# Gate factors made on TensorE, x loaded in three mirrored transfers, masters in blocks of four

## The chip, the cores and the metric

The kernel runs on one core of one Trainium2 chip. The metric is the device time of one launch in microseconds (us). Before the change it is 581.54 us, the median of three runs from 579.77 to 585.35. The profiled run took 580.86 us, and its profile spans 578.8 us from the first to the last instruction.

The engines are called by the profile's short names: PE is TensorE (PEld its weight loads), DVE is VectorE, ACT is ScalarE, POOL is GpSimd, SP is SyncE, which here only issues DMAs (SPq).

## The reference

Two computations on the same x (2048 tokens, 448 features) are mixed by a gate. The first is attention with 16 query heads of 28 and one shared key and value head. The second is a convolution of each feature with a long kernel K that is built from 256 complex modes per feature.

```python
g = sigmoid((x * gate_w).sum(-1, keepdims=True))
# A: attention
q = (x @ wq) in 16 heads of 28;  k = x @ wk;  v = x @ wv
p = softmax(q k^T * 28**-0.5);   a = (p v, heads side by side) @ wo
# B: long convolution
P = exp(dt * A * l), l = 0 .. 2047            # 448 x 256 modes x 2048 positions
K = Re sum_n C[d,n] * dt[d] * B[d,n] * P      # 448 x 2048
b = causal_conv(x, K) per feature, in bf16, + x * Dskip
out = g * a + (1 - g) * b
```

## The kernel before

The program is written as a list of operations with their reads and writes. A scheduler in the Python code orders them per engine with assumed durations (`ns`), priorities (`pr`, lower first) and a `slack` that is added to the assumed arrival of an operand. The order of each engine is then fixed in the program. An engine stalls where the next instruction of its own list isn't ready, even if a later one is.

**Attention.** 1024 score tiles of 128x512 (4 query blocks x 4 head groups x 16 key tiles x 4 heads) come in batches of 3 and 2. PE makes a batch of scores (line 938), ACT takes its exponential (948), PE multiplies with the values (956).

```python
for b in range(nb):                       # nb = 410 batches, 2.5 tiles on average
    if b >= nextc and c < NCH + LAG:
        chunk_step(c)                     # masters, tables(c), kgen(c), conv(c - LAG); LAG = 2
        c += 1; nextc += period
    ...pv(npv)...
    if b + 2 < nb:
        qk(b + 2)
```

After 16 key tiles, `norm` divides by the sum of exponentials. The sums go through DRAM to be spread over partitions: acc (a DVE copy of psB) to denT by DMA, a reciprocal on DVE, denT to R_scratch by DMA, R_scratch to rdenB by four DMAs, and a DVE product into onT. The output projection (885) reads onT.

**Convolution.** The 448 features are 28 chunks of 16. For each chunk DVE builds tables of powers from "masters" (`tables`), PE contracts them to K (`kgen`, 803), DVE packs K into kstg, and a DMA writes it to KP_scratch. Four DMAs of 1 MB (`tload`) read it back as overlapping windows, the Toeplitz data T, in a ring of four slots. PE then multiplies T with U, which holds x in blocks of 64 tokens in reversed block order (`conv`, 864: 128 matmuls for a chunk). DVE scales the result by omq, which is 1 - g in the layout of the reversed convolution, and PE transposes it (842).

```python
def uload(self):
    pg.dma([(U rows 16.., dram(self.Z, ...))], (448, 2048), "uz", rd=["pad", "sw"], wr=["U"], pr=2)   # zeros
    for k in range(3):
        lst = []
        for p in range(16):
            if k == 0: hb, pos, blk = 0, p, 15 - p
            else:      hb, pos, blk = 1, p + 16 * (k - 1), 31 - p - 16 * (k - 1)
            lst.append((U[partitions hb, hb+2, .., 64 of them; columns pos*D .. pos*D+D],
                        dram(x, 64 * blk * D, [[D, 64], [1, D]])))
        pg.dma(lst, (1024, 896), f"u{k}", rd=["sw"], wr=["U"], pr=2)     # 16 DMAs each

def conv(self, c):
    for k in range(4):
        self.tload(4 * c + k)
        for m in range(1, 16, 2):
            pg.op("pe", mm, 112, rd=[("T", s), "U"], ..., slack=2500 if m == 1 else 0)
    pg.op("dve", cst = ps * omq, rd=[X, "omq"]);  self.ytr(c)
```

Every write of U names the same resource, so each of the four groups (zeros, u0, u1, u2) is issued only when the one ahead of it has landed. U is complete only after the last.

**Masters.** For a block of BC chunks, 11 levels of repeated squaring: a copy and a signed copy to bf16 at each level (738, 740), and a square, a subtraction and a product from each level to the next (728, 731, 734). That is 22 + 30 DVE instructions for a block, whatever its size.

```python
sizes = [2, 4, 4, 4, 4, 4, 4, 2]
pr = 50 + c0 if b else 1.4          # masters of the block that starts at chunk c0
# tables of chunk c have pr = 52 + c
```

**Gate operand.** gtok holds g and 1 - g by token. The copy for the convolution's layout goes through DRAM:

```python
pg.op("dve", gb = bf16(1 - g))
pg.dma([(dram(self.G, 0, [[1, P], [P, 16]]), gb)], (2048, 2), "gw", ..., slow=True)   # 2048 elements of 2 bytes
pg.dma([(tq, dram(self.G, 0, [[64, 32], [1, 64]]))], (32, 128), "omq", rd=["G"], wr=[("kst", 1)])
pg.op("pe", mo, 200, rd=["anti", ("kst", 1)], wr=[("b", 5)], slack=6000)   # 2 selector matmuls
pg.op("dve", omq = copy of the result)
```

Of the kernel before, what the change touches and what calls it, by code (L numbers as in the profile page):

```python
# [44 lines left out]
def dram(t, off, dims):  # L45
    return bass.AP(tensor=t.tensor, offset=t.offset + off, ap=[list(d) for d in dims])
# [244 lines left out]
def el(n, rate=0.96, fix=69):  # L291
    return fix + n / rate


class Kernel:
# [4 lines left out]
    def sb(self, name, cols, dt):  # L300
        return Buf(self.es.enter_context(self.nc.sbuf_tensor(name, [P, cols], dt)))
# [23 lines left out]
    def alloc(self):  # L325
        nc = self.nc
        sb = self.sb
        self.psS = self.ps("psS", 3072)
        self.psB = self.ps("psB", 512)
        self.psX = self.ps("psX", 512)  # L330
        self.psSb, self.psBb, self.psXb = self.psS.cast(BF), self.psB.cast(BF), self.psX.cast(BF)
        self.xT = sb("xT", NT * S, BF)
        self.kT = sb("kT", S, BF)
        self.vaug = sb("vaug", 512, BF)
        self.Wq = sb("Wq", NT * 512, BF)
        self.Wk = sb("Wk", NT * P, BF)
        self.Wv = sb("Wv", NT * 32, BF)
        self.Wo = sb("Wo", NT * D, BF)
        self.Wb = sb("Wb", P, BF)
        self.ident = sb("ident", 136, BF)  # L340
        self.absq = sb("absq", 512, BF)
        self.qT = sb("qT", 3 * 512, BF)
        self.expT = sb("expT", 10 * 512, BF)
        self.acc = sb("acc", 2 * 512, F32)
        self.rdenB = sb("rdenB", 512, F32)
        self.denT = sb("denT", 2 * 16, F32)
        self.onT = sb("onT", 6 * 512, BF)
        self.gtok = sb("gtok", 32, F32)
        self.gb = sb("gb", 16, BF)
        self.dskb = sb("dskb", D, BF)  # L350
        self.omq = sb("omq", 128, F32)
        self.anti = sb("anti", 2 * P, BF)
        self.U = sb("U", 32 * D, BF)
        self.O = sb("O", 16 * D, BF)
        self.tab = sb("tab", 2 * 8192, BF)
        self.tmp = sb("tmp", 2 * 2048, BF)
        self.NTR = 4
        self.T = sb("T", self.NTR * 4096, BF)
        sizes = [2, 4, 4, 4, 4, 4, 4, 2]
        self.blocks = [(sum(sizes[:i]), n) for i, n in enumerate(sizes)]  # L360
        self.NB = len(sizes)
        self.BC = max(sizes)
        self.LV = 192
        self.MC = 5 * 192 + 96
        self.mbf = sb("mbf", 2 * self.BC * self.MC, BF)
        BW = self.BC * HC
        self.BW = BW
        self.mst = sb("mst", 2 * 2 * BW, F32)
        self.msq = sb("msq", 2 * BW, F32)
        self.sgn = sb("sgn", 8, F32)  # L370
        self.seedz = sb("seedz", 2 * 2 * D, F32)
        self.seedw = sb("seedw", 2 * 2 * D, BF)
        self.dt32 = sb("dt32", D, BF)
        self.kstg = sb("kstg", 2 * 256, BF)
        self.cst = sb("cst", 2 * 512, BF)
        self.small = sb("small", 32, F32)
        self.zero = sb("zero", 2, BF)
        self.smallb = sb("smallb", 16, BF)
        self.KP = nc.dram_tensor("KP_scratch", (D * KPW,), BF).ap()
        self.Z = nc.dram_tensor("Z_scratch", (1024,), BF).ap()  # L380
        self.G = nc.dram_tensor("G_scratch", (S,), BF).ap()
        self.R = nc.dram_tensor("R_scratch", (16 * 4 * 512,), F32).ap()

    def consts(self):
# [12 lines left out]
        ms = lambda buf, n, val, key, eng="dve": pg.op(eng, lambda e: e.memset(V(buf, 0, n), val), 60 + n / 3.8, wr=[key])  # L397
        pg.op("dve", lambda e: e.memset(V(self.kstg, 0, 256), 0.0), 100, wr=[("kst", 0)])
        ms(self.Wk, NT * P, 0.0, "Wk")
        ms(self.Wq, NT * 512, 0.0, "Wq")  # L400
        ms(self.Wb, P, 0.0, "Wb")
        for hb in range(4):
            pg.op("dve", lambda e, hb=hb: e.memset(self.Wb.v(32 * hb, 28, 32 * hb + 28, [[1, 1]]), -1.0), 60, wr=["Wb"])
        pg.op("dve", lambda e: e.memset(self.vaug.v(0, P, 28, [[32, 16]]), 1.0), 80, wr=["va"])
        pg.op("dve", lambda e: e.memset(self.vaug.v(0, P, 29, [[32, 16], [1, 3]]), 0.0), 80, wr=["va"])
        ms(self.Wo, NT * D, 0.0, "Wo", "pool")
        for z in range(2):
            an = self.anti.v(0, 32, z * P, [[32, 4], [1, 32]])
            pg.op("pool", lambda e, an=an: e.memset(an, 1.0), 100, wr=["anti"], pr=4)
            pg.op("pool", lambda e, an=an, z=z: e.affine_select(out=an, in_=an, compare_op=ALU.is_equal, fill=0.0, base=z - 32,  # L410
                                                                pattern=[[0, 4], [1, 32]], channel_multiplier=1), 300,
                  rd=["anti"], wr=["anti"], pr=4)

    def loads(self):
# [61 lines left out]
    def uload(self):  # L476
        pg, x = self.pg, self.ins["A_x"]
        pg.dma([(bass.AP(tensor=self.U.h, offset=16 * D, ap=[[2 * self.U.rs, 64], [1024, 7], [1, 1024]]),
                 dram(self.Z, 0, [[0, 64], [0, 7], [1, 1024]]))], (448, 2048), "uz", rd=["pad", "sw"], wr=["U"], pr=2)
        for k in range(3):  # L480
            lst = []
            for p in range(16):
                if k == 0:
                    hb, pos, blk = 0, p, 15 - p
                else:
                    hb, pos, blk = 1, p + 16 * (k - 1), 31 - p - 16 * (k - 1)
                lst.append((bass.AP(tensor=self.U.h, offset=hb * self.U.rs + pos * D, ap=[[2 * self.U.rs, 64], [1, D]]), dram(x, 64 * blk * D, [[D, 64], [1, D]])))
            pg.dma(lst, (1024, 896), f"u{k}", rd=["sw"], wr=["U"], pr=2)

    def bank(self, b, bf=False):  # L490
        if b < 6:
# [142 lines left out]
    def prep_gate(self):  # L634
        pg = self.pg
# [15 lines left out]
        pg.op("dve", lambda e: e.tensor_scalar(gv, ov, 0.5, 0.5, ALU.mult, ALU.add), 80, rd=["gt"], wr=["gt"], pr=1.2)  # L651
        pg.op("dve", lambda e: e.tensor_scalar(ov, ov, -0.5, 0.5, ALU.mult, ALU.add), 80, rd=["gt"], wr=["gt"], pr=1.2)
        pg.op("dve", lambda e: e.tensor_copy(self.gb.v(0, P, 0, [[1, 16]]), ov), 80, rd=["gt"], wr=["gb"], pr=1.2)
        pg.dma([(dram(self.G, 0, [[1, P], [P, 16]]), self.gb.v(0, P, 0, [[1, 16]]))], (2048, 2), "gw", rd=["gb"], wr=["G"], pr=3, slow=True)
        tq = self.kstg.v(0, 32, 256, [[1, 64]])
        pg.dma([(tq, dram(self.G, 0, [[64, 32], [1, 64]]))], (32, 128), "omq", rd=["G"], wr=[("kst", 1)], pr=1)
        t, o = self.bank(5)

        def mo(e):
            for z in range(2):  # L660
                r = e.matmul(t.v(0, P, o + 64 * z, [[1, 64]]), self.anti.v(0, 32, z * P, [[1, P]]), tq,
                             start=True, stop=True, tile_position=(0, 0))
            return r
        pg.op("pe", mo, 200, rd=["anti", ("kst", 1)], wr=[("b", 5)], pr=1.7, slack=6000)
        pg.op("dve", lambda e: e.tensor_copy(self.omq.v(0, P, 0, [[1, 128]]), t.v(0, P, o, [[1, 128]])), el(128),
              rd=[("b", 5)], wr=["omq"], pr=1.7)

# [22 lines left out]
    def masters(self, b):  # L690
        pg = self.pg
# [1 line left out]
        BW, MC, B0 = BC * HC, self.MC, c0 * HC  # L693
        W2 = 2 * D
        mo = (b % 2) * self.BC * MC
        pr = 50 + c0 if b else 1.4
        mst, msq, mbf = self.mst, self.msq, self.mbf

        def src(k, comp):
# [152 lines left out]
    def conv(self, c):  # L852
        pg = self.pg
# [3 lines left out]
        for k in range(4):  # L857
# [3 lines left out]
            for m in range(1, 16, 2):  # L861
                def mm(e, k=k, m=m, s=s, gi=gi):
                    for j in range(4):
# [4 lines left out]
                    return r  # L868
                first = k == 0 and m == 1
                pg.op("pe", mm, 112, rd=[("T", s), "U"], wr=[X, ("cst", cs)] + ([("b", 5)] if c == 0 else []) if first else [X], pr=2.5,  # L870
                      lock="C" if first else None, slack=2500 if m == 1 else 0, mode="c32")
        pg.op("dve", lambda e: e.tensor_tensor(self.cst.v(0, P, cs * 512, [[128, 4], [64, 2], [1, 64]]),  # L872
                                               ps.v(0, P, po + 63, [[128, 4], [64, 2], [-1, 64]]),
                                               self.omq.v(0, P, 0, [[0, 4], [64, 2], [1, 64]]), ALU.mult),
# [189 lines left out]
```

## Time and profile before

| what | value |
|---|---|
| time, median of 3 | 581.54 us |
| span of the profile | 578.8 us |
| busy PE / DVE / ACT | 491.5 / 494.6 / 488.9 us |
| exponentials (948) | 410, 472.1 us, 1253 ns each |
| mean granted PE clock | 0.876 |
| DMA moved | 136.6 MB, 236 GB/s over the span |

Three engines are each busy for about 85% of the span. Such shares are averages over a beginning, a long middle and an end with different limits, so the reading goes by stretches of time.

| stretch, us | PE busy | DVE busy | ACT busy | PE clock | DMA share |
|---|---|---|---|---|---|
| 20 to 40 | 14.95 | 17.20 | 17.62 | 0.56 | 0.35 |
| 60 to 80 | 16.54 | 14.88 | 18.49 | 0.67 | 0.31 |
| 80 to 100 | 7.29 | 14.67 | 8.26 | 0.50 | 0.53 |
| 180 to 200 | 17.60 | 20.00 | 20.00 | 1.00 | 0.75 |
| 420 to 440 | 18.05 | 20.00 | 19.70 | 1.00 | 0.92 |
| 540 to 560 | 9.54 | 2.39 | 0.00 | 0.70 | 0.88 |
| 560 to 580 | 6.67 | 4.54 | 0.00 | 0.67 | 0.28 |

### The profile page before, as it was taken

The numbers are of one execution on the slowest core, as the hardware profiler recorded it, in microseconds if no ns is written. First come the engines' busy times: TensorE is split into PE (matmuls) and PEld (weight loads), VectorE is DVE, ScalarE is ACT, GpSimd is POOL, SyncE is SP. The second block draws the span as 40 slices with busy tenths as digits, with TensorE's granted clock in tenths as the row PEclk, the third lists the DMA queues.
The fourth block names the chain that finished last, engine by engine and source line by source line (L and its number), as shares of the span: only waits on it lengthen the run. The fifth ranks groups of instructions, "written<-read, shape, count | busy, mean of one in ns | idle before, by whom it ended". The sixth has DMA issues, their size and how long they took to land.

```text
span 578.8 us, 18479 instructions
## 1 busy us (share of the span) xinstructions
PE 491.5 (85%) x8210; PEld 243.9 (42%) x8210; DVE 494.6 (85%) x1197; ACT 488.9 (84%) x428; POOL 3.7 (1%) x15
## 2 busy tenths in 40 slices
PE   6777962989898999989899999999999989999552
PEld 5411210334444444535345254555544455555431
DVE  4978976799999999999989899999999999992112
ACT  4688891999999999999989799999999989999000
POOL 2000000000000000000000000000000000000000
PEclk9755565779989999979879699999999999989867
DMA  8827336358667778488687667769998868989953
GB/s 227 202 20 58 78 78 203 139 187 310 217 220 297 255 246 286 153 307 296 211 317 213 263 221 255 271 240 337 290 314 298 267 211 324 317 297 302 378 210 127
DMA packets 44847, 136.62 MB, mean 236 GB/s; under 512 B 11516, under 2 KB 27824, under 8 KB 30432
## 3 DMA queue, kind: packets, MB, share of 16 engines
q1 hardware_dynamic: 44032, 135.08, 70.0%
q8 instruction: 64, 1.05, 0.7%
q10 hardware_dynamic: 736, 0.37, 0.2%
q14 instruction: 15, 0.12, 0.1%
HBM read 131.44 MB, written 3.86 MB: 234 GB/s over the span
## 4 chain that ended last, share of the span: by engine, by line
PE 44%; ACT 36%; DMA 9%; DVE 4%; SPq 4%; issue 1%; ACTq 0%
ACT expT L948 35%; PE psS L938 13%; PE psS L864 12%; PE psB L956 8%; PE psX L803 5%; SPq L106 4%; DMA U<-Z_scratch 3%; PE psX L885 2%; PE psX L678 2%; DMA R_scratch<-denT 1%; DMA denT<-acc 1%; PE psS L510 1%; DMA rdenB<-R_scratch 1%; DMA T<-KP_scratch 1%; DVE O L466 1%
## 5 line engine op out<-in xcount | busy, mean ns | idle before, releaser
L948 ACT ACTIVATE expT<-psS 128x1536 bf16<-128x1536 f32 (+1 forms) x410 | 472.1, 1253 | 34.8 <-PE psS L938 19.6
L938 PE MATMUL psS<-qT,kT 29*128 29x512 bf16 x1024 | 174.7, 422 | 36.8 <-ACT expT L948 34.6
L864 PE MATMUL psS<-T,U 128*32 128x128 bf16 (+7 forms) x3584 | 158.4, 303 | 21.1 <-DMA T<-KP_scratch 20.8
L864 PEld LDWEIGHTS psS<-T,U 128*32 128x32 bf16 (+7 forms) x3584 | 114.7, 151 | 56.8 <-issue 27.4
L956 PE MATMUL psB<-expT,vaug 128*32 128x512 bf16 x1024 | 112.0, 428 | 2.3 <-ACT gtok L649 1.3
L938 PEld LDWEIGHTS psS<-qT,kT 29*128 29x128 bf16 x1024 | 39.6, 92 | 135.4 <-ACT expT L948 99.3
L769 DVE TENSOR_TENSOR tab<-tab,mbf 128x128 bf16<-128x128 bf16 (+4 forms) x140 | 78.9, 566 | 0.4
L778 DVE TENSOR_TENSOR tab<-tab,tmp 128x128 bf16<-128x128 bf16 (+4 forms) x140 | 78.5, 566 | 0.4
L772 DVE TENSOR_TENSOR tmp<-tab,mbf 128x128 bf16<-128x128 bf16 (+4 forms) x140 | 78.4, 563 | 0.0
L803 PE MATMUL psX<-tab 128*32 128x96 bf16 x1792 | 58.9, 268 | 2.7 <-issue 2.1
L956 PEld LDWEIGHTS psB<-expT,vaug 128*32 128x32 bf16 x1024 | 26.8, 95 | 68.2 <-issue 63.7
L803 PEld LDWEIGHTS psX<-tab 128*32 128x32 bf16 x1792 | 43.5, 116 | 14.9 <-issue 8.4
L786 DVE TENSOR_TENSOR tab<-tab,mbf 128x2048 bf16<-128x2048 bf16 x28 | 34.1, 1219 | 0.0
L788 DVE TENSOR_TENSOR tab<-tab,mbf 128x2048 bf16<-128x2048 bf16 x28 | 34.0, 1212 | 0.0
L872 DVE TENSOR_TENSOR cst<-psS,omq 128x512 bf16<-128x512 f32 x28 | 19.2, 686 | 13.7 <-PE psS L864 13.7
L740 DVE TENSOR_TENSOR mbf<-mst,sgn 128x256 bf16<-128x256 f32 (+1 forms) x80 | 30.7, 383 | 0.0
L728 DVE TENSOR_TENSOR msq<-mst 128x256 f32<-128x256 f32 (+1 forms) x72 | 27.6, 383 | 0.0
L678 PE MATMUL psX<-xT,Wq 112*128 112x512 bf16 x64 | 24.1, 474 | 0.5 <-DVE qT L687 0.2
L915 DVE TENSOR_TENSOR onT<-acc,rdenB 128x512 bf16<-128x512 f32 x16 | 10.9, 684 | 13.9 <-DMA rdenB<-R_scratch 13.9
L731 DVE TENSOR_TENSOR mst<-msq 128x128 f32<-128x128 f32 (+1 forms) x80 | 21.3, 266 | 0.0
L904 DVE COPY acc<-psB 128x512 f32<-128x512 f32 x16 | 11.0, 688 | 10.3 <-PE psB L956 10.3
L734 DVE SCALAR_TENSOR_TENSOR mst<-mst 128x128 f32<-128x128 f32 (+1 forms) x72 | 19.2, 267 | 0.0
(100 smaller groups left out, 251.3 us busy)
## 6 DMA issues: line engine op xcount, KB each, us to landing
T<-KP_scratch SPq DMA_DIRECT2D x112, 1024.0 KB, 7.9
rdenB<-R_scratch SPq DMA_DIRECT2D x64, 64.0 KB, 3.2
U<-in_A_x_dram SPq DMA_DIRECT2D x48, 56.0 KB, 2.2
tab<-in_A_x_dram SPq DMA_DIRECT2D x4, 448.0 KB, 6.6
O<-in_A_x_dram SPq DMA_DIRECT2D x1, 1792.0 KB, 9.8
KP_scratch<-kstg SPq DMA_DIRECT2D x28, 64.0 KB
out_dram<-O SPq DMA_DIRECT2D x16, 112.0 KB, 1.8
U<-Z_scratch SPq DMA_DIRECT2D x1, 896.0 KB, 15.2
```

The costliest lines, as they stand in the source:

```text
L678: pg.op("pe", lambda e, T=T: e.matmul(px, self.Wq.v(0, DT, T * 512 + g * 128, [[1, 128]]), self.xT.v(0, DT, T * S + 512 * qc, [[1, 512]]), ...
L740: pg.op("dve", lambda e, k=k, io=io, sg=sg: e.tensor_tensor(mbf.v(0, P, mo + io, [[MC, BC], [1, 64]]), src4(k), self.sgn.v(0, P, sg, [[0, ...
L769: pg.op("dve", lambda e, d=dst, a=src, m=m, w=w: e.tensor_tensor(d, a, mbf.v(0, P, m, [[4, 16], [0, 2 * w], [1, 4]]), ALU.mult), el(n, 1.9 ...
L772: pg.op("dve", lambda e, a=src, m=m, w=w: e.tensor_tensor(tmp.v(0, P, so, [[4 * w, 32], [1, 4 * w]]), a, mbf.v(0, P, m + 64, [[4, 32], [0, ...
L778: pg.op("dve", lambda e, d=d2, t=t2: e.tensor_tensor(d, d, t, ALU.add), el(n, 1.92), rd=[("tmp", s), ("tab", s, lv + 1)], wr=[("tab", s, l ...
L786: pg.op("dve", lambda e: e.tensor_tensor(ua, src, mbf.v(0, P, m, [[4, 8], [0, 64], [1, 4]]), ALU.mult), el(2048, 1.92), rd=rk + mk, wr=[(" ...
L788: pg.op("dve", lambda e: e.tensor_tensor(ub, src, mbf.v(0, P, m + 32, [[4, 16], [0, 32], [1, 4]]), ALU.mult), el(2048, 1.92), rd=rk + mk, ...
L803: r = e.matmul(self.psX.v(32 * g, 32, 96 * jj, [[1, 96]]), tab.v(0, P, qp + 2048 + o, [[4, 32]]), tab.v(0, P, to + o, [[2048, 3], [4, 32]] ...
L864: r = e.matmul(ps.v(32 * j, 33 - m, po + 128 * k, [[1, 128]]), self.U.v(0, P, (m - 1) * D + 4 * gi + j, [[D, 33 - m]]), self.T.v(0, P, s * ...
L938: r = e.matmul(self.psS.v(0, P, 1536 * s + 512 * k, [[1, 512]]), kT.v(32 * h, DH + 1, 128 * kt, [[1, 128]]), qT.v(32 * h, DH + 1, 512 * qs ...
L948: pg.op("act", lambda e: e.activation(expT.v(0, P, 512 * (i0 % 10), [[1, n]]), self.psS.v(0, P, 1536 * s, [[1, n]]), AF.Exp, scale=SQ), 75 ...
L956: r = e.matmul(self.psB.v(32 * h, 32, 0, [[1, 512]]), vaug.v(0, P, 32 * kt, [[1, 32]]), expT.v(0, P, 512 * ((4 * st + h) % 10), [[1, 512]] ...
```

## The change

Three things change together.

1. The gate operand no longer goes through DRAM. PE transposes gb (128 x 16) into 16 rows, DVE copies them to kstg, and four selector matmuls (16 rows instead of 32, two halves that accumulate) make omq. Two DMAs fall away. POOL builds four selectors instead of two.
2. The 48 DMAs that load x into U become three, with a block axis that runs backwards through U.
3. The masters come in seven blocks of four instead of eight of 2, 4, ..., 4, 2, and those after the first rank later, just before the tables of their first chunk. In the scheduler, the assumed lateness of T for the first convolution chunk rises from 2.5 to 9 us, so that the chunk is placed later.

```diff
-        self.anti = sb("anti", 2 * P, BF)
+        self.anti = sb("anti", 4 * P, BF)
-        sizes = [2, 4, 4, 4, 4, 4, 4, 2]
+        sizes = [4] * 7
-        self.G = nc.dram_tensor("G_scratch", (S,), BF).ap()
... (consts: four selectors with 16 rows and a row step of 2 instead of two with 32 rows)
+        rs = self.U.rs
         for k in range(3):
-            lst = []
-            for p in range(16):
-                if k == 0:
-                    hb, pos, blk = 0, p, 15 - p
-                else:
-                    hb, pos, blk = 1, p + 16 * (k - 1), 31 - p - 16 * (k - 1)
-                lst.append((bass.AP(tensor=self.U.h, offset=hb * self.U.rs + pos * D, ap=[[2 * self.U.rs, 64], [1, D]]), dram(x, 64 * blk * D, [[D, 64], [1, D]])))
-            pg.dma(lst, (1024, 896), f"u{k}", rd=["sw"], wr=["U"], pr=2)
+            hb, p0, b0 = (0, 15, 0) if k == 0 else (1, 31, 0) if k == 1 else (1, 15, 16)
+            pg.dma([(bass.AP(tensor=self.U.h, offset=hb * rs + p0 * D, ap=[[2 * rs, 64], [-D, 16], [1, D]]),
+                     dram(x, 64 * b0 * D, [[D, 64], [64 * D, 16], [1, D]]))], (1024, 896), f"u{k}", rd=["sw"], wr=["U"], pr=2)
...
-        pg.dma([(dram(self.G, 0, [[1, P], [P, 16]]), self.gb.v(0, P, 0, [[1, 16]]))], (2048, 2), "gw", rd=["gb"], wr=["G"], pr=3, slow=True)
-        tq = self.kstg.v(0, 32, 256, [[1, 64]])
-        pg.dma([(tq, dram(self.G, 0, [[64, 32], [1, 64]]))], (32, 128), "omq", rd=["G"], wr=[("kst", 1)], pr=1)
+        tq = self.kstg.v(0, 16, 256, [[1, P]])
+        tb, ob = self.bank(5, True)
+        pg.op("pe", lambda e: e.matmul(tb.v(0, 16, ob, [[1, P]]), self.gb.v(0, P, 0, [[1, 16]]), self.ident.v(0, P, 0, [[1, P]]),
+                                       is_transpose=True, tile_position=(0, 0)), 100, rd=["gb", "id"], wr=[("b", 5)], pr=1.6)
+        pg.op("dve", lambda e: e.tensor_copy(tq, tb.v(0, 16, ob, [[1, P]])), el(P), rd=[("b", 5)], wr=[("kst", 1)], pr=1.2)
...
             for z in range(2):
-                r = e.matmul(t.v(0, P, o + 64 * z, [[1, 64]]), self.anti.v(0, 32, z * P, [[1, P]]), tq,
-                             start=True, stop=True, tile_position=(0, 0))
+                for half in range(2):
+                    r = e.matmul(t.v(0, P, o + 64 * z, [[1, 64]]), self.anti.v(0, 16, (2 * z + half) * P, [[1, P]]),
+                                 self.kstg.v(0, 16, 256 + 64 * half, [[1, 64]]),
+                                 start=(half == 0), stop=(half == 1), tile_position=(0, 0))
-        pg.op("pe", mo, 200, rd=["anti", ("kst", 1)], wr=[("b", 5)], pr=1.7, slack=6000)
+        pg.op("pe", mo, 300, rd=["anti", ("kst", 1)], wr=[("b", 5)], pr=1.7)
...
-        pr = 50 + c0 if b else 1.4
+        pr = 51.5 + c0 if b else 1.4
... (conv)
-                      lock="C" if first else None, slack=2500 if m == 1 else 0, mode="c32")
+                      lock="C" if first else None, slack=(2500 if gi else 9000) if m == 1 else 0, mode="c32")
```

More of the change, by code (lines that the diff above doesn't have):

```diff
@@ L406, in consts @@
         ms(self.Wo, NT * D, 0.0, "Wo", "pool")
-        for z in range(2):
-            an = self.anti.v(0, 32, z * P, [[32, 4], [1, 32]])
+        for zh in range(4):
+            an = self.anti.v(0, 16, zh * P, [[32, 4], [1, 32]])
             pg.op("pool", lambda e, an=an: e.memset(an, 1.0), 100, wr=["anti"], pr=4)
-            pg.op("pool", lambda e, an=an, z=z: e.affine_select(out=an, in_=an, compare_op=ALU.is_equal, fill=0.0, base=z - 32,
-                                                                pattern=[[0, 4], [1, 32]], channel_multiplier=1), 300,
+            pg.op("pool", lambda e, an=an, zh=zh: e.affine_select(out=an, in_=an, compare_op=ALU.is_equal, fill=0.0,
+                                                                  base=zh // 2 + zh % 2 - 32, pattern=[[0, 4], [1, 32]],
+                                                                  channel_multiplier=2), 300,
                   rd=["anti"], wr=["anti"], pr=4)
```

## The prediction

> **What bounds the kernel now.** I read four views, in this order: the waits by engine, the timelines of SP and PE around the longest of them, the busy times by stretch, and the chain of work at the end.
>
> ```profile
> ACT expT L948 <- PE psS L938: 19.6, 18, 11.6
> SPq L106 <- DMA G_scratch<-gb: 13.0, 1, 13.0
> ```
>
> The columns of the waits are the sum in us, the number and the longest. ACT waited for scores for 19.6 us in all, and 11.6 us of it in one piece. SP stood for 13 us behind the write of the gate to DRAM.
>
> ```profile
> 36.74 0.38 SPq L106 DMA_DIRECT2D G_scratch<-gb  x1
> 39.64 0.67 SPq L106 DMA_DIRECT2D U<-Z_scratch  x1
> 53.38 0.32 SPq L106 DMA_DIRECT2D kstg<-G_scratch  x1
> 54.90 22.35 SPq L106 DMA_DIRECT2D U<-in_A_x_dram  x32
> 77.29 0.68 SPq L106 DMA_DIRECT2D denT<-acc  x1
> 78.75 10.90 SPq L106 DMA_DIRECT2D U<-in_A_x_dram  x16
> 89.69 0.59 SPq L106 DMA_DIRECT2D KP_scratch<-kstg  x1
> 92.22 0.56 SPq L106 DMA_DIRECT2D T<-KP_scratch  x1
> ```
>
> This is SP's timeline (start, duration, instruction). SP is a serial resource here: the gate and the 48 small loads of x keep it from 36.7 to 89.7 us. The first K (KP_scratch) can be written only then, although DVE had packed it at 72.2 us (end of the copy at line 818), and the first T follows.
>
> ```profile
> 86.57 0.61 PE L938 MATMUL psS<-qT,kT 29*128 29x512 bf16 x2
> 98.41 1.22 PE L864 MATMUL psS<-T,U 128*32 128x128 bf16 x32 [11.24 <-DMA T<-KP_scratch]
> ```
>
> In PE's own order the first convolution matmul comes next, and its T isn't there. PE stops, no scores are made, and ACT stops from 88.6 to 100.2 us. This is the hole in the stretch from 80 to 100 us.
>
> ```profile
> 40.00:50.00 10.00, 8.95 (x8) 0.50 0.91 46
> 390.00:400.00 10.00, 9.98 (x10) 1.00 0.95 351
> ```
>
> These are the exponentials by stretch: length, ACT busy, granted PE clock, DMA share, GB/s. From 100 to 536.6 us they fill the time almost wholly: that stretch has about 419 us of them and some 17 us of gaps. The DMA engines at 40 us are as busy as at 390 us, but for an eighth of the bytes: this is the gate's write of 2-byte elements, with the zeros of U beside it.
>
> ```profile
> 537.84 5.65 DMA denT<-acc
> 543.79 7.68 DMA R_scratch<-denT
> 552.30 1.34 SPq L106
> 553.69 6.79 DMA rdenB<-R_scratch
> 560.50 0.70 DVE onT L915
> ```
>
> This is the end of the chain. After the last exponential (536.6 us) 42.2 us remain: three dependent DMAs, which share the queues with the last 1 MB loads of T, then the last projection and the stores.
>
> **What the Trainium skill says.** "DMA: Bandwidth & Descriptors", section Specifications, puts the smallest efficient transfer at 512 B and says that below it a read-modify-write is done. The trace agrees: 4 KB in 2-byte elements held SP for 13.0 us. The same page, section "Issuing engines are not separate DMA queues", says that issuing costs sequencer time, usually small beside the DMA. Here it isn't small: 32 issues took 22.35 us, 0.70 each, for 56 KB that land in 2.2 us. "TensorE: Matmul & The Clock Gate", Part 1, says that the clock is halved until PE has been busy for a window. The trace shows 0.50 to 0.67 before the convolution starts and 1.00 in most later stretches, so that the stretch before the first convolution chunk is slow for PE in both kernels.
>
> **The change part by part.**
>
> *The loads of x.* 48 issues (22.35 + 10.90 us) become three. One load of x into O, 1.8 MB in pieces of the same 896 B, landed in 9.8 us by the table of DMA issues. Half of that with its fixed part is 5 to 6 us, so I estimate 6 us for each of the three, one after the other. With the zeros landed at 54.9 us or earlier, U is complete at about 73 us instead of 91.
>
> *The gate.* Two DMAs and the 13 us wait go. Added are five small matmuls of under 0.5 us each at half clock and one DVE copy of about 0.2 us, at a time when PE waits for ACT anyhow: I count 0.5 us.
>
> *The masters.* By the groups kept apart by shape, a block of two costs 11x0.189 + 11x0.284 + 10x0.284 + 10x0.216 + 10x0.217 = 12.4 us of DVE. A block of four costs 11x0.220 + 11x0.416 + 10x0.416 + 10x0.282 + 10x0.284 = 16.8 us. Two blocks of two go and one of four comes: 8.0 us less in all. But the first block grows by 4.4 us and stands ahead of the first tables. In PE's built order the first K is contracted after score tile 95 instead of 80.
>
> *When the first T is there.* The old hole came after tile 115, with the exponentials reaching 88.6 us. Before it, 36 exponentials ran from 43.42 to 88.61 us, 1.26 us each, or 0.50 us a tile. Tile 95 is thus reached at about 78.5 us. The write of K takes 0.6 us to issue and 2.5 us to land (89.69 to 92.22), four rdenB issues stand beside it (2.3 us), and the first T took 6.2 us from 92.22 to 98.4. So T is there at about 88 us. The convolution now starts after tile 135, which is 20 tiles or 8 exponentials later: 88.6 + 8x1.26 = 98.7 us. It finds U and T ready, with 10 us to spare.
>
> *The middle.* Before, the 909 tiles after tile 115 took 536.6 - 88.6 - 11.6 = 436.4 us, 0.480 us each. At the same pace 889 tiles end at 98.7 + 426.8 = 525.5 us. That is 11.1 us earlier.
>
> *The tail.* The built orders differ here as well. After the last product with the values, 320 convolution matmuls were left, now 256. After the last denT transfer, six loads of T were left, now four, and only one of them, instead of three, stands between R_scratch and the four rdenB. At the 344 GB/s of the stretch from 540 to 560 us a load of 1.05 MB takes 3.05 us, so up to 6.1 us are to be had. The writing of R_scratch still has three loads ahead of it, so I take two thirds, 4 us.
>
> *Sum.* 11.1 for the hole, 4 for the tail, less 0.5 for the added gate work and 0.6 for gaps that move: 14 us. 581.5 - 14 = 567.5 us.
>
> **The rivals.** First, another wait takes the place of the hole. The first K is contracted later, and the loads of U now run as three dependent transfers of 0.9 MB into 64 partitions with a backward axis. If one of these took 15 us, as the zeros did, U would be there only at 100 us, at the planned start of the convolution. For this speaks that nobody has seen that transfer; against it, that the zeros shared the engines with the gate's write. It would give 575 to 581 us. Second, the middle is bound by more than ACT. From 140 to 520 us DVE is idle for about 10 us only and PE for some 25, and the same convolution work must fit into 889 tiles instead of 909. The masters, now placed just before the tables of their first chunk, could make K come in bursts. For it speaks the built order: K for chunks 3 and 4 is contracted at tiles 185 and 245, with 60 tiles between. Against it: DVE has 8 us less work and no longer loses the 9 us (3.80 and 5.33) that it spent before 100 us on denT and rdenB. If the pace fell from 0.480 to 0.490 us, 9 us would go: 575 to 577. Third, the tail is a chain of latencies and doesn't shrink: 571 to 572. In the other direction, if R_scratch also passes sooner and some gaps of the middle close, 560.
>
> **Range and chances.** The hole is the surest part. The tail is worth 0 to 6 us and the middle is uncertain by some 6 us either way. I put 8 in 10 on 559 to 577 us. The line of 2% is at 569.9 us, a little above my value, so: faster 0.63, same 0.33, slower 0.04.
>
> **What would show it.** Right: no wait of ACT above 3 us near 100 us; the first convolution matmul at 96 to 101 us with no DMA as its releaser; SP free of U's loads before 75 us; the last exponential at 523 to 529 us; 37 to 40 us from there to the end; about 486 us of DVE. Wrong: a wait on U or T ahead of the first convolution matmul; more than 22 us of gaps between the exponentials after it; a tail of 42 us or more; or a clock that stays at half after 100 us.

## The result

| kernel | median | range | ratio to before, 95% interval |
|---|---|---|---|
| before | 581.88 us (4 runs) | 579.77 to 585.35 | |
| after | 552.96 us (4 runs) | 552.07 to 554.21 | 0.9499 [0.9448, 0.955] |

The change saves 28.9 us, twice the 14 us that were predicted, and 552.96 us lies below the range of 559 to 577 us. The profiled executions span 578.8 and 552.4 us, so they show 26.4 us of it.

SP's timeline of the kernel after (start, duration, instruction):

```profile
41.20 0.68 SPq L106 DMA_DIRECT2D U<-Z_scratch  x1
49.07 11.41 SPq L106 DMA_DIRECT2D U<-in_A_x_dram  x3
66.71 0.66 SPq L106 DMA_DIRECT2D denT<-acc  x1
...
79.13 0.58 SPq L106 DMA_DIRECT2D KP_scratch<-kstg  x1
79.76 1.86 SPq L106 DMA_DIRECT2D rdenB<-R_scratch  x4
81.72 2.81 SPq L106 DMA_DIRECT2D T<-KP_scratch  x4
```

SP no longer stands behind the gate. The zeros land in 7.9 us by the table of DMA issues instead of 15.2, each of the three loads of x in 5.4 us, and U is complete at about 66 us at the latest (the third is issued by 60.5 us). SP still waits for one load before it issues the next, as the 11.41 us for three issues show. The first K is written at 79.1 us, the four loads of T follow from 81.7. PE's timeline at the first convolution matmul of after:

```profile
96.08 0.39 PE L938 MATMUL psS<-qT,kT 29*128 29x512 bf16 x2
96.40 0.48 PE L864 MATMUL psS<-T,U 128*32 128x128 bf16 x8
```

There is no bracket with a releaser: PE waits for nothing, and the hole is gone. The waits of ACT in the kernel after (sum in us, number, longest):

```profile
ACT expT L948 <- PE psB L956: 9.6, 27, 0.9
ACT expT L948 <- PE psS L938: 3.7, 8, 0.9
```

The wait for scores fell from 19.6 to 3.7 us. That is 4 us more than the 11.6 us of the hole. The waits after 100 us, for scores and for the products with the values (psB), fell as well. First before, then after, both from 100 us to the last exponential (the 11.6 us in the first view are the hole, which ends at 100.2 us):

```profile
ACT expT L948 <- PE psS L938: 17.9, 15, 11.6
ACT expT L948 <- PE psB L956: 9.8, 26, 1.5
```

```profile
ACT expT L948 <- PE psB L956: 7.3, 22, 0.7
ACT expT L948 <- PE psS L938: 0.8, 3, 0.5
```

Without the hole, the 16.1 us of short waits after 100 us became 8.1 us. The groups of instructions say that the exponentials themselves are the same in both kernels; before, then after (busy us, mean ns, idle time ahead of them):

```profile
L948 ACT ACTIVATE expT<-psS 128x1536 bf16<-128x1536 f32 (+1 forms) x410 | 472.1, 1253 | 34.8 <-PE psS L938 19.6
```

```profile
L948 ACT ACTIVATE expT<-psS 128x1536 bf16<-128x1536 f32 (+1 forms) x410 | 470.0, 1252 | 14.2 <-PE psB L956 9.6
```

The chain that ended last, in after (start, duration, work):

```profile
519.69 9.60 DMA R_scratch<-denT
...
531.62 2.15 DMA rdenB<-R_scratch
533.77 0.02 issue
533.79 0.70 DVE onT L915
...
534.54 5.62 PE psS L885 x16
540.16 1.03 PE psS L864 x24
```

The last exponential ends at 514.4 us, and rdenB, which took 6.79 us, now takes 2.15.

The end of the exponentials can be written as a sum for every kernel here: 40 us, ACT's busy time after it (460 to 463 us in all of them), and ACT's idle time. Then comes a tail. I worked out this table from the exponentials' timeline and the busy times by stretch of one profile each; it says where time went, and the medians below say how much. The gaps after 100 us differ by some 3 us between profiles of one order: 12.7 to 15.8 us in hole_closed and in the run that shortens DVE's products in its order, and in the order of after 8.8 us in after and 12.0 in two_store_queues, which changes only the stores at the end. A step of 3 us or less in this column is not resolved by one profile.

| kernel | ACT idle, 40 to 100 us | ACT idle, 100 us to last exponential | last exponential ends | tail | span |
|---|---|---|---|---|---|
| before | 16.1 | 17.9 | 536.6 | 42.2 | 578.8 |
| hole_closed | 6.6 | 12.7 | 520.8 | 43.6 | 564.4 |
| hole_closed_warm | 6.4 | 18.9 | 528.1 | 41.7 | 569.8 |
| hole_closed_full | 6.2 | 13.0 | 521.4 | 41.7 | 563.1 |
| hole_closed_dve_minus | 6.1 | 15.8 | 523.5 | 41.9 | 565.4 |
| loads_only | 6.6 | 9.6 | 517.8 | 40.6 | 558.4 |
| gate_only | 12.8 | 13.7 | 528.7 | 42.4 | 571.1 |
| masters_only | 11.6 | 17.0 | 530.5 | 40.7 | 571.2 |
| no_masters | 5.1 | 11.4 | 518.9 | 41.0 | 559.9 |
| old_sizes | 4.8 | 11.3 | 517.5 | 38.5 | 556.0 |
| old_rank | 4.4 | 7.9 | 513.0 | 43.5 | 556.5 |
| after | 4.7 | 8.8 | 514.4 | 38.0 | 552.4 |
| dve_plus | 4.5 | 14.4 | 520.8 | 37.8 | 558.6 |
| dve_minus_big | 4.6 | 7.7 | 512.3 | 37.1 | 549.4 |

From before to after: 11.4 us of idle time around the hole, 9.1 us of gaps after it, 1.7 us of ACT busy time and 4.2 us of tail, 26.4 in all.

### The profile page after: what moved, and what is told of

It is laid out like the page before. It is cut to its first block, busy times and chain, and to the rows that moved or that the text cites. A ratio compares the mean times of both kernels' runs of the same rounds, so it can differ in the third digit from the quotient of the medians.

```text
span 552.4 us, 18386 instructions
## 1 busy us (share of the span) xinstructions
PE 483.9 (88%) x8213; PEld 243.9 (44%) x8213; DVE 489.1 (89%) x1146; ACT 486.7 (88%) x428; POOL 4.7 (1%) x19
## 4 chain that ended last, share of the span: by engine, by line
PE 40%; DVE 30%; ACT 21%; DMA 5%; POOL 1%; issue 1%; SPq 0%; POOLq 0%
ACT expT L948 20%; PE psS L938 12%; PE psS L864 10%; PE psB L956 7%; DVE tmp L772 5%; DVE tab L769 5%; DVE tab L778 4%; PE psX L803 4%; DMA T<-KP_scratch 3%; DVE tab L786 2%; PE psX L885 2%; DVE tab L788 2%; DMA R_scratch<-denT 2%; DVE mbf L740 1%; PE psX L678 1%; PE psS L506 1%
## 5 line engine op out<-in xcount | busy, mean ns | idle before, releaser
L938 PE MATMUL psS<-qT,kT 29*128 29x512 bf16 x1024 | 172.2, 416 | 34.0 <-ACT expT L948 32.2
L938 PEld LDWEIGHTS psS<-qT,kT 29*128 29x128 bf16 x1024 | 39.6, 92 | 130.5 <-ACT expT L948 101.4
L769 DVE TENSOR_TENSOR tab<-tab,mbf 128x1024 bf16<-128x1024 bf16 (+4 forms) x140 | 79.2, 568 | 0.4
L778 DVE TENSOR_TENSOR tab<-tab,tmp 128x1024 bf16<-128x1024 bf16 (+4 forms) x140 | 79.1, 569 | 0.5
L772 DVE TENSOR_TENSOR tmp<-tab,mbf 128x1024 bf16<-128x1024 bf16 (+4 forms) x140 | 79.2, 569 | 0.0
L740 DVE TENSOR_TENSOR mbf<-mst,sgn 128x256 bf16<-128x256 f32 x70 | 29.6, 423 | 0.0
L728 DVE TENSOR_TENSOR msq<-mst 128x256 f32<-128x256 f32 x63 | 26.6, 422 | 0.0
L678 PE MATMUL psX<-xT,Wq 112*128 112x512 bf16 x64 | 21.2, 428 | 0.9 <-DVE kstg L818 0.8
L731 DVE TENSOR_TENSOR mst<-msq 128x128 f32<-128x128 f32 x70 | 20.2, 289 | 0.0
L734 DVE SCALAR_TENSOR_TENSOR mst<-mst 128x128 f32<-128x128 f32 x63 | 18.3, 290 | 0.0
L738 DVE CAST mbf<-mst 128x128 bf16<-128x128 f32 x70 | 15.8, 225 | 0.0
```

What stands on the lines that cost most here:

```text
L678: pg.op("pe", lambda e, T=T: e.matmul(px, self.Wq.v(0, DT, T * 512 + g * 128, [[1, 128]]), self.xT.v(0, DT, T * S + 512 * qc, [[1, 512]]), ...
L740: pg.op("dve", lambda e, k=k, io=io, sg=sg: e.tensor_tensor(mbf.v(0, P, mo + io, [[MC, BC], [1, 64]]), src4(k), self.sgn.v(0, P, sg, [[0, ...
L769: pg.op("dve", lambda e, d=dst, a=src, m=m, w=w: e.tensor_tensor(d, a, mbf.v(0, P, m, [[4, 16], [0, 2 * w], [1, 4]]), ALU.mult), el(n, 1.9 ...
L772: pg.op("dve", lambda e, a=src, m=m, w=w: e.tensor_tensor(tmp.v(0, P, so, [[4 * w, 32], [1, 4 * w]]), a, mbf.v(0, P, m + 64, [[4, 32], [0, ...
L778: pg.op("dve", lambda e, d=d2, t=t2: e.tensor_tensor(d, d, t, ALU.add), el(n, 1.92), rd=[("tmp", s), ("tab", s, lv + 1)], wr=[("tab", s, l ...
L938: r = e.matmul(self.psS.v(0, P, 1536 * s + 512 * k, [[1, 512]]), kT.v(32 * h, DH + 1, 128 * kt, [[1, 128]]), qT.v(32 * h, DH + 1, 512 * qs ...
```

## The experiments

All times are medians, with the ratio to the kernel before in runs on the same chip. I began with two theories: the gains are the hole and what each part of the change adds; or the large part comes from a change of order in the middle. Later theories are told where they arise. Line numbers differ by a few between the kernels: L938, L935 and L943 are the same product.

### One part at a time

**hole_closed** is the kernel before with each group of 16 loads of x made one DMA, while the scheduler still counts 16, so that every instruction keeps its place.

```diff
-            for p in range(16):
-                ... lst.append((... [[2 * self.U.rs, 64], [1, D]] ..., [[D, 64], [1, D]]))
-            pg.dma(lst, ..., pr=2)
+            pg.dma([(... [[2 * rs, 64], [-D, 16], [1, D]] ..., [[D, 64], [64 * D, 16], [1, D]])], ..., pr=2, nd_sched=16)
```

> The kernel before with its instruction order untouched on every engine; only each group of 16 small loads of x is one transfer. Theory A (two separate gains: the hole near 90 us, and half-clock episodes later that come from the order): U is complete near 73 us, the hole of 11.6 us goes, the half-clock episodes at 285 to 295 and 320 to 330 us come back 11 to 12 us earlier at the same score tiles. About 570 us, ratio 0.98. Rival B (the later gaps were an after-effect of the hole): the later gaps go as well, about 560 us.

567.84 us, 0.9775 [0.972, 0.9829]: 13 us for the loads alone, in an unchanged order, where the interval allows 10 to 16. The hole is gone (its row in the table: 9.5 us less idle time before 100 us) and 5.2 us of the later gaps with it, or as little as 2 if the 15.8 us of hole_closed_dve_minus in the same order are taken. The result lies between the two theories and nearer to the first: the stretches at half clock came back, as shown further down.

**loads_only** is the same with the scheduler told the truth, so that it reorders.

```diff
-            pg.dma([...], ..., pr=2, nd_sched=16)
+            pg.dma([...], ..., pr=2)
```

> The kernel before with the three loads of x, gate through DRAM kept, and the order made anew by the scheduler. The hole goes (-11.6 us). If the half-clock episodes near 290 and 325 us belong to the old order alone, they go or shrink too: 562 to 566 us. If they belong to the old masters: 568 to 570 us.

562.42 us, 0.9671 [0.9618, 0.9725]: the new order is worth another 5 us or so, of which the profiles show 3.1 us as gaps and 3.0 in the tail. Median and gaps each lie at the edge of what the runs resolve.

**gate_only** takes the transposes and selector matmuls and leaves the 48 loads.

```diff
-        pg.dma([(dram(self.G, ...), self.gb ...)], ..., "gw", ...)
-        pg.dma([(tq, dram(self.G, ...))], ..., "omq", ...)
+        pg.op("pe", lambda e: e.matmul(tb ..., self.gb ..., self.ident ..., is_transpose=True, ...), ...)
+        pg.op("dve", lambda e: e.tensor_copy(tq, tb ...), ...)
```

> The kernel before with the gate operand made on PE, the 48 loads of x kept. The zeros of U land some 6 us earlier, because the 2-byte write is gone, and the gate's 13 us wait on SP goes, but 48 issues of 0.7 us remain: U complete near 84 us, the hole shrinks from 11.6 to 3 to 6 us. 572 to 577 us if nothing else moves; the new order may add or take 5.

572.78 us, 0.9832 [0.9765, 0.9899]. SP's timeline of gate_only:

```profile
41.28 0.67 SPq L106 DMA_DIRECT2D U<-Z_scratch  x1
48.92 35.66 SPq L106 DMA_DIRECT2D U<-in_A_x_dram  x48
84.62 0.65 SPq L106 DMA_DIRECT2D KP_scratch<-kstg  x1
```

The 13 us wait of SP is gone, but the 48 issues still hold SP until 84.6 us, and the first K is only 5.1 us earlier than before. A hole of 8.8 us stays:

```profile
ACT expT L953 <- PE psS L943: 14.7, 12, 8.8
```

The gate alone saves 3.3 us of idle time before 100 us and 4.2 us of gaps after it, in an order that the scheduler made anew.

**masters_only** is the kernel before with seven blocks of four and the later rank; **no_masters** is the kernel after without either.

```diff
-        sizes = [2, 4, 4, 4, 4, 4, 4, 2]
+        sizes = [4] * 7
-        pr = 50 + c0 if b else 1.4
+        pr = 51.5 + c0 if b else 1.4
```

> The kernel before with only the masters changed (seven blocks of four, ranked later). Theory D (the new placing of the masters gives the pace of the middle): the hole stays at 8 to 12 us, the half-clock episodes of the middle go, 572 to 576 us. If the masters matter only with the hole closed: 580 us.

> The changed kernel with the old masters (eight blocks, old rank). Theory D: the hole is closed, the middle is as bad as before, the tail in between: 564 to 570 us. Rival B (all follows from the hole): 553 to 557 us.

572.87 us, 0.9852 [0.9799, 0.9905], and 561.03 us, 0.9657 [0.9597, 0.9716]. The masters save 8 to 9 us in either setting, the rest 20 to 21 us: two nearly additive parts. Only the totals agree: in masters_only the largest piece is 4.5 us of idle time before 100 us, at the hole; from no_masters to after, where there is no hole, it is 3.0 us of tail and 2.6 us of gaps. Against loads_only (0.9671), no_masters (0.9657) adds the gate and the later placing of the first convolution chunk, and the two can't be told apart: the gate, worth 1.7% alone, shows no gain of its own once the loads are three. The prediction gave the masters nothing of their own. Waits of ACT in masters_only:

```profile
ACT expT L948 <- PE psS L938: 15.5, 12, 9.1
```

The hole is still there, as it should be, with 9.1 us.

**old_rank** and **old_sizes** split the masters: after with only the rank, or only the sizes, put back (one line of the diff above each).

> The changed kernel with blocks of four and the old, earlier rank of the masters. Theory E (only DVE's work counts): 553 to 555 us. Theory F (placing counts): 556 to 560 us.

> The changed kernel with the eight old blocks and the new, later rank. Theory E: 560 to 562 us, as with the old masters altogether. Theory F: 553 to 557 us.

559.71 us, 0.9627 [0.9591, 0.9662], and 557.91 us, 0.96 [0.9564, 0.9635]. Both count (6.7 and 4.9 us), and not additively, as together they are worth 8. In the table old_rank has even less idle time than after, and its whole loss is the tail, 43.5 us instead of 38.0. Its chain at the end:

```profile
519.60 7.58 DMA R_scratch<-denT
...
528.50 8.95 DMA rdenB<-R_scratch
...
537.48 0.70 DVE onT L915
538.23 4.90 PE psS L885 x16
543.13 2.01 PE psS L864 x54
```

Against the chain of after, rdenB takes 8.95 us instead of 2.15, as loads of T run beside it, and 54 convolution matmuls are left after the last projection instead of 24. So with the later rank less convolution work and fewer loads of T are left for the tail; how this comes about among DVE's instructions wasn't followed.

### Is it the PE clock?

In hole_closed the granted clock falls twice in the middle, as it does before. Busy times by stretch of hole_closed (length, then PE, PEld, DVE, ACT and POOL busy with their counts, clock, DMA share, GB/s):

```profile
270.00:280.00 10.00, 8.38 (x92) 2.88 (x89) 9.30 (x15) 9.27 (x9) 0.00 (x0) 0.76 0.96 364
310.00:320.00 10.00, 9.53 (x95) 3.50 (x95) 8.25 (x18) 7.50 (x7) 0.00 (x0) 0.69 0.45 165
```

In the second stretch PE is busy for 9.53 of 10 us at a clock of 0.69, and the exponentials get only 7.50. The old order has no convolution matmul between score tiles 500 and 515 and between 565 and 580. Two kernels fill these places, both with products that nobody reads: **hole_closed_warm** repeats the first score product of a batch twice (29 of 128 rows of the array), **hole_closed_full** adds one product over all 128 rows.

```diff
+ if k == 0 and (500 <= first[b] < 516 or 563 <= first[b] < 580):   # hole_closed_warm
+     for _ in range(2): r = e.matmul(..., kT.v(32 * h, DH + 1, ...), qT.v(32 * h, DH + 1, ...), ...)
+ if k == 0 and (495 <= first[b] < 520 or 560 <= first[b] < 585):   # hole_closed_full
+     e.matmul(..., kT.v(0, P, ...), qT.v(0, P, ...), ...)
```

> As the run with the hole closed, same order, and the first score matmul of each batch is repeated twice in two thin stretches (score tiles 500 to 516 and 563 to 580), which adds about 13 x 2 x 0.21 = 5.5 us of PE work and changes no result. Theory A (PE is idle there, its clock falls to half, and the slow PE then starves ACT): the clock stays at 1.00, the gaps of ACT around these tiles shrink from about 7 us to 3, and the run is 3 to 5 us faster than with the hole closed alone. Rival C (the gaps come from the order and from operands that arrive late): no faster, or slower by the added work.

> The kernel with the hole closed, same order, and one extra matmul ahead of each score batch in the two thin stretches (20 in all, score tiles 495 to 520 and 560 to 585). Unlike the repeated scores, which use 29 of the 128 rows of PE, it uses all 128 rows and columns (about 20 x 0.22 = 4.4 us of PE work; its output is overwritten by the scores, no result changes). Theory A (the clock follows how much of the array works, and the half clock then starves ACT): the clock stays at 1.00 from 265 to 325 us, the gaps of ACT there fall from about 5 us to under 2, and the time is 3 to 5 us below the 567.8 us of the hole closed. Rival C (the gaps come from the order itself): the clock may stay up, but the time doesn't fall, or rises by up to 4 us.

572.73 us, 0.9866 [0.9788, 0.9945], and 566.33 us, 0.9743 [0.9687, 0.98]. The same stretch in hole_closed_warm, then in hole_closed_full:

```profile
310.00:320.00 10.00, 9.53 (x76) 2.72 (x79) 5.46 (x16) 6.46 (x6) 0.00 (x0) 0.54 0.63 253
```

```profile
310.00:320.00 10.00, 10.00 (x118) 4.33 (x118) 9.36 (x19) 9.10 (x9) 0.00 (x0) 1.00 0.47 164
```

Products over a quarter of the rows didn't hold the clock and cost some 5 us. Full ones, which also begin a few tiles sooner and end a few later, held it at 1.00 and brought ACT from 7.50 to 9.10 us in this stretch. But the whole time differs from hole_closed by 1.5 us, within both intervals, and the gaps after 100 us are 13.0 us against 12.7. The added products take PE time themselves (the next score product starts some 0.32 us later), so this run shows the sum of their cost and the clock's gain. The clock is real and local; it isn't shown to carry the missing microseconds. Late loads of T don't either: in before, hole_closed and loads_only no wait of PE for T shows between 100 us and the last exponential, and 0.2 us in after.

### Is it DVE?

DVE is busy for 20.00 of 20 us in most stretches of the kernel after, so I formed the theory that DVE, not ACT, bounds the middle, and that the masters' smaller work pays directly. **dve_plus** adds 24 reductions of 256 elements to the masters' steps of the kernel after, each instruction otherwise in its place.

```diff
+ if b and k in (2, 4, 6, 8):
+     e.tensor_reduce(self.dum.v(0, P, j, [[1, 1]]), src_both(k - 1), AX.X, ALU.max)
  return e.tensor_tensor(msq ..., src_both(k - 1), src_both(k - 1), ALU.mult)
```

> The changed kernel, order untouched on every engine, with 24 reductions of 256 elements added to DVE beside the masters (24 x 0.34 = 8.2 us, the work that the new blocks save; their results are not used). Theory E (the masters part is worth 8 us because DVE is the bound of the middle): 559 to 562 us. Theory F (DVE has slack, the gain of the masters lies in where the order puts the convolution): 553 to 555 us.

561.53 us, 0.9678 [0.9629, 0.9727]: 7.3 us more DVE work (496.4 instead of 489.1 us busy) cost 8.6 us. This spoke for the theory. **skip_pool** was to show the other sign, with the 16 skip products moved to GpSimd. **skip_pool_norm_act** also takes back the later placing of the first convolution chunk and issues the last three small DMAs from ACT:

```diff
-  pg.op("dve", lambda e ...: e.scalar_tensor_tensor(ov, ov, gtok, dskb, ALU.mult, ALU.mult), ...)
+  pg.op("pool", lambda e ...: e.tensor_tensor(ov, ov, dskb, ALU.mult), ...)
+  pg.op("pool", lambda e ...: e.tensor_scalar(ov, ov, gtok, None, ALU.mult), ...)
```

> The kernel after, with the 16 skip products (O times the gate times Dskip, 448 elements, 0.68 us each on DVE by the groups, 10.8 us in all) made on GpSimd, as two instructions each. Theory, DVE's work is the bound of the middle: DVE busy falls by 8 to 11 us up to the last K pack, and the time falls nearly as much, to 543 to 547 us. Rival, ACT bounds the middle and DVE only follows it: DVE busy falls as much, its idle time grows by the same, and the time stays at 551 to 554 us. In between (547 to 551) another engine takes over within a few us.

> As skip_pool, with the slack of the later tables at 2500 instead of 9000 (worth nothing by itself so far), and with the three small DMAs of the last normalisation (denT, R_scratch, rdenB) issued by ACT instead of SP. If the 49 us after the last K pack are set by these DMAs standing behind the 1 MB loads of T in SP's queue, the rest falls by 3 to 6 us and the time is that much below skip_pool. If the DMA engines themselves are shared with the loads, or the last projections set the end, the time is within 1.5 us of skip_pool.

571.96 us, 0.9831 [0.9787, 0.9875], and 570.53 us, 0.9841 [0.9784, 0.9897]: neither theory's number. Two things went wrong with the experiment. DVE's timeline in skip_pool, while GpSimd works:

```profile
68.23 1.21 DVE L770 TENSOR_TENSOR tab<-tab,mbf 128x2048 bf16<-128x2048 bf16 x1
69.37 2.04 DVE L773 TENSOR_TENSOR tmp<-tab,mbf 128x2048 bf16<-128x2048 bf16 x1
...
74.63 1.21 DVE L787 TENSOR_TENSOR tab<-tab,mbf 128x2048 bf16<-128x2048 bf16 x1
75.76 2.05 DVE L789 TENSOR_TENSOR tab<-tab,mbf 128x2048 bf16<-128x2048 bf16 x1
```

Products of the same size take 1.21 us or 2.05, where after has a mean of 1.22: GpSimd holds DVE up. And the copy of the gate waited for GpSimd, which skip_pool's waits show, so that a new hole opened:

```profile
DVE gb L470 <- POOL O L468: 6.4, 1, 6.4
```

**dve_minus** and **dve_minus_big** repeat it without GpSimd. The last two products of each table are made shorter, from chunk 2 on, in the same places: one of the two with 1536 elements, or both with 1024. They leave a part of the tables unmade.

```diff
-        ua = tab.v(0, P, to, [[1, 2048]])
-        ub = tab.v(0, P, to + 2048 + 128, [[256, 8], [-128, 2], [1, 128]])
+        na, nb = (6, 8) if c > 1 else (8, 8)          # dve_minus_big: (4, 4)
+        ua = tab.v(0, P, to, [[1, 256 * na]])
+        ub = tab.v(0, P, to + 2048 + 128, [[256, nb], [-128, 2], [1, 128]])
```

> The kernel after, every instruction at its old place; only the first of the two last products of each table is cut from 2048 to 1536 elements for the chunks from 2 on (26 instructions of 1.22 us, about 0.27 us less each: 7 us less DVE work, and a quarter of that table isn't made). Theory, DVE bounds the middle: 5 to 7 us faster than after, 546 to 548 us. Rival, ACT bounds it: 551 to 554 us, with DVE's idle time grown by the 7 us.

> As dve_minus, with both last products cut to 1024 elements (52 instructions, about 0.55 us less each: 28 us less DVE work). Then ACT must bound: at most its 13.5 us of idle time can go. Theory: 8 to 12 us faster than after, 541 to 545 us, DVE idle for 25 us or more and ACT for under 6 us. Rival, ACT bounds already: 551 to 554 us.

552.45 us, 0.9502 [0.947, 0.9534], and 553.22 us, 0.9518 [0.9474, 0.9562]: the same time as after, for 5.3 and 24.1 us less DVE work. Busy times from 100 to 500 us, first after, then dve_minus_big, then dve_plus:

```profile
100.00:500.00 400.00, 376.10 (x7035) 197.82 (x7036) 395.07 (x935) 391.45 (x343) 0.00 (x0) 0.98 0.78 275
```

```profile
100.00:500.00 400.00, 376.35 (x7070) 198.57 (x7066) 370.84 (x934) 392.59 (x344) 0.00 (x0) 0.99 0.78 277
```

```profile
100.00:500.00 400.00, 371.63 (x6888) 194.02 (x6888) 398.05 (x954) 385.85 (x336) 0.00 (x0) 0.98 0.76 270
```

With less work DVE falls from 395 to 371 us and ACT stays at 392 of 400. With more, DVE stays full and ACT falls to 386. The theory falls: ACT bounds the kernel after, and DVE stands within a few us of it, so that here the work added to DVE cost its full time and the work removed from it brought nothing. The two also touch different places, the masters' steps and the ends of the tables; whether the place has a part in it wasn't tried.

That leaves the old order, where ACT has larger gaps. **hole_closed_dve_minus** shortens the same products as dve_minus_big, in hole_closed.

> hole_closed (the kernel before with only the hole taken out, every instruction at its old place), with the two last products of each table cut to 1024 elements for the chunks from 2 on, as in dve_minus_big: about 24 us less DVE work, a part of the tables isn't made. In the kernel after the same cut gained nothing: there ACT is the bound. Here ACT still has 12.7 us of gaps after 100 us instead of 8.8. Theory, these gaps come from DVE's work arriving late in the old order: they fall to about 8 us and the time by 3 to 5 us against hole_closed, to 563 to 565 us, ratio 0.967 to 0.972. Rival, they come from PE's order and its clock (the stretches at half clock around score tiles 500 and 570): the gaps stay at 11 to 13 us and the time at 566 to 569 us, ratio 0.974 to 0.980.

568.28 us, 0.9794 [0.9746, 0.9842] (6 runs): the same as hole_closed, though DVE is idle for 51.0 us from 40 us to the last exponential instead of 24.1. Its gaps after 100 us are 15.8 us instead of 12.7, so they didn't shrink either. The gaps of the old order are not DVE's. What is left is the order of PE's own work with its stretches at half clock. How much of this is order and how much clock stays open.

### The tail

**slack_2500** takes back the later placing of the first convolution chunk (the assumed lateness of its T is 2.5 us again instead of 9), which bears on the start and not on the tail; it stands here with the other runs on the kernel after. **two_store_queues** issues every second store from ACT, and **last_norm_act** issues the three small DMAs of the last normalisation from ACT, away from SP's loads of T. All three start from the kernel after.

```diff
-  slack=(2500 if gi else 9000) if m == 1 else 0            # slack_2500
+  slack=2500 if m == 1 else 0
+  ... f"out{i}", rd=["O"], pr=1, eng="act" if i % 2 else "sp")   # two_store_queues
+  qe = "act" if i == 15 else "sp"                            # last_norm_act, for denT, R_scratch and rdenB
```

> The changed kernel without the later placing of the first convolution chunk, which then comes after score tile 123 instead of 135. By the changed kernel's trace T is there at about 90 us, and tile 123 is reached at 91 to 92 us: no hole, or one under 2 us. 552 to 556 us. If T is late: a hole of 3 us or more near 90 us, 556 to 558 us.

> The changed kernel with every second store of the output issued from ACT, which is idle at the end, instead of all 16 from SP (7.7 us of issuing). 8 issues of 0.48 us on each side end 3 to 4 us earlier: 549 to 550 us against 553. If the stores wait for the DMA engines and not for their issue: no change.

> The kernel after, with the three small DMAs of the last normalisation issued by ACT instead of SP, so that they don't stand behind the six last 1 MB loads of T. If SP's queue sets the tail, 38 us after the last exponential become 32 to 35 and the time 547 to 550 us. If the T loads and the convolution after them set the end, the time stays at 551 to 554 us.

551.48 us, 0.9488 [0.9454, 0.9523]; 553.45 us, 0.9514 [0.9455, 0.9572]; 552.93 us, 0.9522 [0.9471, 0.9574]. None can be told from after, so the assumed 9 us are worth nothing measurable. The chain at the end of last_norm_act shows why its new queue brought nothing:

```profile
515.48 14.12 DMA denT<-acc
...
529.62 0.26 DVE denT L912
...
529.91 1.46 DMA R_scratch<-denT
...
532.70 2.01 DMA rdenB<-R_scratch
```

denT is 8 KB. It was issued at once, but took 14.12 us while five loads of 1 MB from SP landed, three of which were issued after it. The two steps after them then took 1.46 and 2.01 us. The wait isn't in SP's queue but in the DMA engines; it only moved from R_scratch (9.60 us in after) to denT. No version here beats the kernel after beyond its interval.

## Why the prediction was wrong

- *The loads of x.* Right in kind, and too slow: U was ready some 7 us sooner than the 73 us, and each load took 5.4 us instead of 6. The zeros were assumed at 54.9 us as before; without the gate's write beside them they landed in half the time.
- *The gate, and the first T.* Right. No new wait at U or T; the first convolution matmul stands at 96.4 us (96 to 101 predicted), and the exponentials reach tile 135 at 98.2 us (98.7 predicted). Rival one didn't happen.
- *The middle.* This is the step that failed: "At the same pace 889 tiles end at 98.7 + 426.8 = 525.5 us." They ended at 514.4 us. From tile 135 on, 889 tiles took 416.2 us, 0.468 us each instead of 0.480. The step took the pace of before over whole, and so kept all gaps between exponentials after the hole as if they belonged to the work. They fell from 17.9 to 8.8 us, and ACT's busy time by 1.7: 10.8 of the 11.1 us. By one profile each, 5.2 us of the gaps go with the hole in an unchanged order (hole_closed), 3.1 more with the reordering that the loads bring (loads_only), and 0.8 is left for the gate and the masters together. Their single effects don't add up (the gate alone takes 4.2 us, the sizes 2.5 from old_sizes to after), and the split is no finer than some 3 us. That the gaps close is shown; why the new orders have fewer of them, by order or by clock, stays open. The view was right that ACT bounds (dve_minus_big), and the prediction's rival "some gaps of the middle close, 560" named the direction but not the size.
- *The masters.* The step computed "8.0 us less in all" for DVE and gave it no place in the sum. DVE's busy time fell by 5.5 us. The masters are worth 8 to 9 us of the whole, and not all of it as saved DVE time: the rank, which takes no work from DVE, is worth 6.7 us, seen in the tail, and the sizes 4.9. dve_plus shows that DVE stands at the balance, where the longer masters could cost; whether old_sizes loses by that or by its order is not separated.
- *The tail.* Predicted 4 us, measured 4.2, and by the cause that was named: fewer loads of T ahead of rdenB, which fell from 6.79 to 2.15 us. The writing of R_scratch took 9.60 us instead of 7.68, so that the net figure is partly luck. old_rank takes it back.
- *The rivals.* The second feared a slower pace, because DVE and PE are nearly full. It had the right fact, DVE near its limit, and the wrong sign. The third, a tail that doesn't shrink, didn't happen.

## What to carry to other kernels

Write the end as the bounding engine's busy time plus its gaps, and treat the gaps as part of the schedule, not of the pace: here a change that reorders closed half of them, in places it never touches. When two engines stand within a few per cent of each other, test both signs: here work added to the second cost in full, and work taken from it brought nothing. A part that pays alone may pay nothing beside another: the gate was worth 1.7% alone, and with the loads in place its gain could not be told from zero.

## What the hardware showed

- The clock depends on more than PE's busy time. In hole_closed_warm PE was busy for 9.53 of 10 us with products over 29 of 128 rows and got a clock of 0.54; in hole_closed_full, with some products over all rows among them, 1.00 at 10.00 us busy. The kernel before had 0.52 at 9.84 us busy (320 to 330 us). The Trainium skill ("TensorE: Matmul & The Clock Gate", Part 1) ties the clock to how busy PE has been recently; here busy time alone doesn't predict it. That the rows in use decide is not shown: the two runs also differ in where their products stand.
- DVE products from two inputs in SBUF took up to 0.84 us longer (1.21 and 2.05 us) while GpSimd worked in SBUF. "GPSIMD Engine Reference", 1. Specifications, says that the two contend for such instructions, and the trace agrees.
- 4 KB written in 2-byte elements doubled the landing of another transfer: the zeros of U took 15.1 to 15.4 us in four kernels that write the gate to DRAM (before, hole_closed, loads_only, masters_only), and 7.6 to 7.9 in gate_only, no_masters and after.
- An 8 KB transfer from another engine's queue took 14.12 us while five 1 MB loads from SP landed (last_norm_act).
